# One queue for all transfers, the first four units' factors spread by TensorE, ScalarE's table loaded first

## The chip, the cores and the metric

The kernel runs on one core of a Trainium2 chip. The metric is the time of one execution on the device in microseconds; three runs of the kernel before are given, and one more execution was recorded by the hardware profiler. Engines are named as the profile names them: PE is TensorE (PEld its weight loads), DVE is VectorE, ACT is ScalarE, POOL is GpSimd, SP is SyncE. SPq and ACTq are the instruction queues of SP and ACT where they issue transfers.

## What is computed

A chunked linear-attention scan over 4 batches, 8 heads and 768 positions feeds two feed-forward layers with weights given in float64.

```python
# attention, per batch and head, chunk by chunk
log_a = np.log(np.clip(a, 1e-06, 1.0))
...
M = CB * L                      # L: products of the factors a between j and i, causal
y_intra = np.einsum('bhij,bhjd->bhid', M, xc)
y_inter = np.einsum('bhin,bhnd->bhid', Cc, state) * decay_to_i[:, :, :, None]
y[:, :, sl] = y_intra + y_inter
state = decay_full[:, :, None, None] * state + np.sum(Bx, axis=2)
...
# layer 1: rms norm, gate and value (256 -> 1536), silu(g) * val @ w_out (1536 -> 256)
silu = g * (1.0 / (1.0 + np.exp(-g)))
return (silu * val @ w_out).astype(np.float32)
...
# layer 2: 256 -> 2048 -> 256
g = s * (r * r) + b             # r = relu(x @ w_in)
return (g @ w_out).astype(np.float32)
```

## The kernel before

The attention works in 32 **units**. A unit is one chunk of 48 positions for two batches (two batches of one pair; unit number c is step c // 2 of pair c % 2), all heads, on 128 partitions. Each unit passes five steps: `scan` (DVE builds the decay products of the factors a into `a_sb`), `gram` (32 small PE matmuls from `raw_bc` into `y`, then DVE multiplies by the decays into `m`), `outs` (32 small PE matmuls of `m` with the inputs `xh`, then ACT copies to `yt`), `back` (PE transposes `yt`, ACT hands the state rows to the unit two later and squares, DVE and POOL make the norm factor `rs`, the scaled rows go to `xn`) and `turn` (PE transposes `xn`; the columns land in `xth`, and, from block 1 on, also in `xtl`). Four units make a block of 384 tokens, and there are eight blocks.

The weights arrive as float64 and are decoded on the chip: 12 tiles `w1[m]` of 768 KB (`load1`, `decode1`) and 16 tiles `w2[m]` of 512 KB (`decode2`). A decode is five DVE instructions and two ACT activations (the names `e`, `sg`, `raw`, then `w1f`). Buffers for raw `w1` tiles are three, so the load of tile m+3 waits for the decode of tile m.

Block 0 runs through layer 1 in plain float32 while the weights arrive (`hidden1_plain`): for tile i the first half of the block's columns (units 0 and 1) is taken as soon as the tile is decoded, and the second half (units 2 and 3) three tiles later. All later phases use three matmuls per product on a split into high and low parts.

What orders the work is a planner, the class `Plan`. Every instruction is recorded (`add`, with its dependences); `issue` then runs a list scheduler over all engines with prices from `price`, and writes the instructions out engine by engine in the order found. All computing instructions stand on one line, 306, in the profile; tiles tell them apart. Where the planner sees a hole on PE before the first layer-1 output it fills it with `idle` matmuls on a constant (line 302).

Transfers have two queues: SP's for most, and ACT's for the weight tiles and for the first `raw_bc` loads of units 0 and 1 (`load_bc`, `load1`, `decode2`). A transfer issued on ACT stands in ACT's own instruction order, so ACT does nothing else while one waits. The transfers of both queues share eight completion counters (DMAHW0 to DMAHW7 in the order rows below), taken in turn; a transfer waits on its counter until the earlier one on it has landed.

The factors reach a unit's partitions in three ways. Units 0 and 1 (`NCLIP = 2`) load raw factors broadcast over 64 partitions (`raw_a`, 128 KB each, two per unit) and clip them on DVE. At the same time all factors are loaded once into `a_cl`, clipped, and written to the scratch `a_scr` in HBM. Units 2 and 3 load theirs broadcast from `a_scr` (98 KB each, two per unit), later units in transfers for two steps at a time (196 KB).

Of the kernel before, what the change touches and what calls it, by code (L numbers as in the profile page):

```python
# [19 lines left out]
P = 128  # L20
# [3 lines left out]
NH = 8  # L24
# [4 lines left out]
NPAIR = 2  # L29
NUNIT = CPB * NPAIR  # L30
SLOTS = 2 * NPAIR
AW = CH + 1
# [6 lines left out]
DM = 256  # L39
NCLIP = 2  # L40
SIZE = {F32: 4, F32R: 4, I32: 4, U32: 4, BF16: 2, I16: 2, U16: 2, I64: 8}
# [11 lines left out]
class Plan:  # L53
# [18 lines left out]
    def __init__(self, nc):  # L72
        self.nc, self.ops, self.clock, self.pace = nc, [], 0.0, False
        self.seen, self.rings, self.masks, self.before = {}, {}, {}, {}
        self.closed, self.sent = set(), None
        for e in ("tensor", "vector", "scalar", "gpsimd", "sync"):
            setattr(self, e, Engine(self, e))

    def add(self, eng, fn, args, kw):
        op = dict(eng=eng, fn=fn, args=args, kw=kw, preds={}, paced=self.pace, i=len(self.ops))  # L80
        op["dur"] = self.price(eng, fn, args, kw)
        if fn == "dma_start":
            op["eng"] = "dma" if eng == "sync" else "words"
        reads = [a for k, a in kw.items() if k not in self.WRITES] + list(args)
        writes = [a for k, a in kw.items() if k in self.WRITES]
        if args and fn in self.FIRST_OUT:
            writes.append(reads.pop(len(kw) - len(writes)))
        for a in reads:
            self.touch(op, a, False)
        for a in writes:  # L90
            self.touch(op, a, True)
        if op["eng"] == "words":

            if self.sent is not None:
                op["preds"].setdefault(self.sent["i"], -self.DMA_LEAD - self.sent["dur"])
            self.sent = op
        op["clock"] = self.clock
        op["group"] = kw["out"].name if fn == "matmul" and not self.pace else None
        if self.pace:
            self.clock += op["dur"]  # L100
        self.ops.append(op)
# [45 lines left out]
    def need(self, op, o):  # L147
        if o is not op:
            lag = 0.0 if o["eng"] == op["eng"] == "tensor" else self.SEM_OF.get(o["eng"], self.SEM)
            op["preds"][o["i"]] = lag + (self.DMA_TAIL if o["eng"] in ("dma", "words") else 0.0)  # L150

# [35 lines left out]
    def queue_of(self, op):  # L187
        return "scalar" if op["eng"] == "words" else op["eng"]


    def forward(self, succs, late):
# [12 lines left out]
        def able(i):  # L204
            return max(ready[i], flights[-self.FLIGHTS]) if ops[i]["eng"] in ("dma", "words") else ready[i]

        for _ in ops:
# [6 lines left out]
            if pick is None:  # L214
                for n, i in enumerate(queue):
                    if able(i) > now + 1e-9:
                        continue
                    end = now + (self.DMA_ISSUE if ops[i]["eng"] == "words" else self.lasts(ops[i], now))
                    if e == "dma" or not any(
# [10 lines left out]
            start[pick] = now  # L230
            if op["eng"] in ("dma", "words"):
# [19 lines left out]
    def backward(self, succs, start, end):  # L251
# [8 lines left out]
        for _ in ops:  # L260
# [3 lines left out]
            free[e] = now + ops[i]["dur"]  # L264
            done = free[e] + (self.DMA_LEAD if e in ("dma", "words") else 0.0)
            late[i] = end - done
# [6 lines left out]

    def issue(self, idle):
        ops = self.ops
# [17 lines left out]
        _, start, stop = min(found, key=lambda f: f[0])  # L293

        ones = self.nc.const_aps.tensor(1.0, (P, P), BF16)
        until = min(start[op["i"]] for op in ops if getattr(op["kw"].get("out"), "name", None) == idle.name)
        busy = self.BEGIN
        for op in sorted(ops, key=lambda o: (start[o["i"]], o["i"])):
            i = op["i"]
            if op["eng"] == "tensor" and start[i] <= until:  # L300
# [3 lines left out]
                busy = stop[i]  # L304
            engine = getattr(self.nc, {"dma": "sync", "words": "scalar"}.get(op["eng"], op["eng"]))
            getattr(engine, op["fn"])(*op["args"], **op["kw"])  # L306
# [13 lines left out]
def scan_glu_relu2(ctx: ExitStack, tc: tile.TileContext, bc, xr, aa, cst, w1, w2, gn, sv, bv, out):  # L320
# [29 lines left out]
    mhalf, emin = fixed[:, 0:1], fixed[:, 1:2]  # L350
    a_cl = att1.tile([P, 4, R], F32, tag="yt", name="a_cl")
    a_scr = dram.tile([2 * NUNIT, NH * AW], F32, name="a_scr")
# [11 lines left out]
    def load_a(c):  # L364
        step, p = c // NPAIR, c % NPAIR
        t = a_t[c] = a_sb[:, c % SLOTS]
        for z in range(2):
            rows = slice(z * R, (z + 1) * R)
            if c < NCLIP:
                if z == 0:  # L370
                    raw = att2.tile([P, NH, R], F32, tag="m", name="raw_a")
                    nc.gpsimd.memset(t[:, :, 0:1], 0.0)
                nc.sync.dma_start(out=raw[rows].rearrange("p h r -> p (h r)"),
                                  in_=aa[chunk(c, z)].partition_broadcast(R))
            elif step == 1:
                nc.sync.dma_start(out=t[rows].rearrange("p h r -> p (h r)"),
                                  in_=a_scr[chunk(c, z)].partition_broadcast(R))
            elif step % 2 == 0:
                src = a_scr[chunk(c, z)]
                nc.sync.dma_start(  # L380
                    out=a_sb[rows, p::NPAIR].rearrange("p s h r -> p s (h r)"),
                    in_=bass.AP(src.tensor, src.offset, [[0, R], [NH * AW, 2], [1, NH * AW]]),
                )
        if c < NCLIP:
            clip_a(t[:, :, 1:AW], raw[:, :, 1:AW])
# [361 lines left out]

    o_t[0, 1] = new_o()
    tokens_to(1)
    for c in range(NPAIR):  # L750
        load_bc(c)
        load1(c)
    clip_a(a_cl[:, :, 1:AW], a_cl[:, :, 1:AW])
    nc.sync.dma_start(out=a_scr.rearrange("c (u h r) -> (c u) h r", u=2, h=4), in_=a_cl[:, :, 0:AW])
# [36 lines left out]
    with tc.manual_schedule():  # L791
        nc.issue(o_t[0, 1][0][:, :P])

# [70 lines left out]
```

## Time and profile before

| | us |
|---|---|
| three runs: lowest, median, highest | 682.12, 685.0, 685.35 |
| the profiled execution, its own time | 682.58 |
| its span, first to last instruction | 680.8 |
| PE busy | 657.7 (97%) |
| DVE busy | 390.6 (57%) |
| ACT busy | 351.8 (52%) |
| DMA moved | 36.14 MB, mean 53 GB/s |

The profiled execution's own time is 1.78 us above its span. Matmuls are pipelined and their ends are modelled, so "PE busy" says that PE had work, not that it worked at its peak. The `idle` matmuls count as busy.

### The profile page before, as it was taken

To read this page: it belongs to the slowest core of one execution; us is meant where nothing else is said; L and a number is where in the kernel's file an instruction comes from. 1 tells how busy PE (TensorE), PEld (TensorE's weight loads), DVE (VectorE), ACT (ScalarE), POOL (GpSimd) and SP (SyncE) were. 2 spreads that over 40 slices of the span, in tenths; PEclk is the share of its full clock that TensorE was granted. 3 is DMA by queue.
4 is the path that set the end of the run, shared out by engine and by line. 5 is a ranking of instruction groups with operands and counts; after the bars stand their busy time and mean duration, and the time that the engine had idled before them with its cause. 6 is when DMAs were issued, how large, how long until landed. Compare 5 with 4: busy or idle time off the path is not lost.

```text
span 680.8 us, 14058 instructions
## 1 busy us (share of the span) xinstructions
PE 657.7 (97%) x5569; PEld 630.8 (93%) x5569; DVE 390.6 (57%) x849; ACT 351.8 (52%) x790; POOL 34.7 (5%) x90
## 2 busy tenths in 40 slices
PE   4689999999999999999999999999999999999997
PEld 3579989899999989999999989999899999999997
DVE  2679999999944573345633465344733454334343
ACT  0778745876645553356533564345533554344553
POOL 3010010100000010000100010000100000000000
PEclk9999999999999999999999999999999999999999
DMA  6796792400001030001200031000400000000000
GB/s 143 206 206 231 230 264 106 97 6 0 7 1 25 7 92 24 0 7 29 73 22 1 7 95 26 1 7 7 92 24 1 6 2 25 1 1 1 4 21 25
DMA packets 26962, 36.14 MB, mean 53 GB/s; under 512 B 13840, under 2 KB 21008, under 8 KB 26896
## 3 DMA queue, kind: packets, MB, share of 16 engines
q1 hardware_dynamic: 22480, 16.89, 10.8%
q10 hardware_dynamic: 4416, 18.35, 8.6%
q8 instruction: 44, 0.72, 0.4%
q14 instruction: 22, 0.18, 0.1%
HBM read 31.98 MB, written 3.25 MB: 52 GB/s over the span
## 4 chain that ended last, share of the span: by engine, by line
PE 89%; DMA 6%; DVE 2%; ACT 1%; issue 1%; SPq 0%; ACTq 0%; POOL 0%; DVEq 0%; POOLq 0%
PE h L306 49%; PE o L306 34%; PE y L306 6%; DMA raw<-in_w 3%; DMA raw_a<-in_aa 1%; DMA a_sb<-a_scr 1%; DMA a_cl<-in_aa 1%; DVE a_sb L306 0%; SPq L306 0%; DVE m L306 0%; ACT L306 0%; ACT sg L306 0%; ACT s L306 0%; DVE e L306 0%; PE o L302 0%
## 5 line engine op out<-in xcount | busy, mean ns | idle before, releaser
L306 ACT ACTIVATE s<-h 128x384 f32<-128x384 f32 x212 | 104.4, 492 | 161.0 <-PE h L306 101.7
L306 PE MATMUL h<-x,w2hl 128*128 128x384 f32 x768 | 164.1, 341 | 0.0
L306 DVE TENSOR_TENSOR lo<-s,hi 128x384 fp32r<-128x384 f32 x212 | 118.0, 557 | 48.2 <-ACT hi L306 37.6
L306 PEld LDWEIGHTS h<-x,w2hl 128*128 128x128 f32 x768 | 135.9, 188 | 1.3
L306 PE MATMUL o<-hi,w2hl 128*128 128x384 f32 (+1 forms) x512 | 133.6, 342 | 0.0
L306 PE MATMUL h<-xtl,w1h 128*128 128x384 f32 x336 | 113.9, 340 | 0.9 <-DVE xtl L306 0.8
L306 PE MATMUL h<-xth,w1h 128*128 128x384 f32 x336 | 114.7, 341 | 0.0
L306 PE MATMUL h<-xth,w1l 128*128 128x384 f32 x336 | 113.7, 338 | 0.0
L306 DVE CAST hi<-s 128x384 fp32r<-128x384 f32 x128 | 45.8, 358 | 104.5 <-ACT s L306 91.5
L306 DVE TENSOR_TENSOR s<-h,s 128x384 f32<-128x384 f32 x84 | 46.7, 556 | 80.7 <-PE h L306 80.7
L306 PEld LDWEIGHTS o<-hi,w2hl 128*128 128x128 f32 x512 | 91.6, 188 | 1.2
L306 PE MATMUL o<-lo,w2hl 128*128 128x384 f32 (+1 forms) x256 | 87.8, 344 | 0.0
L306 ACT CAST hi<-s 128x384 fp32r<-128x384 f32 x84 | 43.1, 513 | 75.9 <-DVE s L306 75.7
L306 ACT ACTIVATE s<-s 128x384 f32<-128x384 f32 x128 | 67.2, 525 | 3.8
L306 PEld LDWEIGHTS h<-xtl,w1h 128*128 128x128 f32 x336 | 63.1, 188 | 1.8 <-DVE xtl L306 1.8
L306 PEld LDWEIGHTS h<-xth,w1h 128*128 128x128 f32 x336 | 63.1, 188 | 0.8 <-DVE h L306 0.2
L306 PEld LDWEIGHTS h<-xth,w1l 128*128 128x128 f32 x336 | 63.1, 188 | 0.2
L306 PE MATMUL o<-hi,w1h 128*128 128x384 f32 x168 | 57.1, 340 | 0.8 <-ACT hi L306 0.8
L306 PE MATMUL o<-hi,w1l 128*128 128x384 f32 x168 | 57.0, 339 | 0.0
L306 PE MATMUL o<-lo,w1h 128*128 128x384 f32 x168 | 56.9, 339 | 0.0
L306 POOL TENSOR_TENSOR rs<-ss,fixed 128x1 f32<-128x1 f32 x32 | 26.0, 811 | 461.2 <-DVE ss L306 461.2
L306 PEld LDWEIGHTS o<-lo,w2hl 128*128 128x128 f32 x256 | 48.1, 188 | 0.9
(65 smaller groups left out, 720.0 us busy)
## 6 DMA issues: line engine op xcount, KB each, us to landing
raw<-in_w ACTq DMA_DIRECT2D x12, 768.0 KB, 6.6
raw<-in_w ACTq DMA_DIRECT2D x16, 512.0 KB, 6.3
a_sb<-a_scr SPq DMA_DIRECT2D x28, 196.0 KB, 4.1
raw_bc<-in_bc SPq DMA_DIRECT2D x56, 64.0 KB, 3.8
xh<-in_xr SPq DMA_DIRECT2D x64, 48.0 KB, 3.0
out_t<-ob SPq DMA_DIRECT2D x14, 192.0 KB, 2.4
raw_a<-in_aa SPq DMA_DIRECT2D x4, 128.0 KB, 4.1
raw_bc<-in_bc ACTq DMA_DIRECT2D x8, 64.0 KB, 3.6
```

The costliest lines, as they stand in the source:

```text
L306: getattr(engine, op["fn"])(*op["args"], **op["kw"])
```

## The change

Four things are done.

1. Every transfer is issued by SP. `load_bc`, `load1` and `decode2` use `nc.sync`; the planner has one transfer queue "dma" in place of "dma" and "words". The weight tiles keep their order among themselves (`words` with the flag `turns`).
2. The first four units (`NCLIP = 2 * NPAIR`) take their factors from the one clipped tile `a_cl`: `spread_a` issues four PE matmuls per unit (out 64x196, the stationary operand a column of `ident` broadcast to 64 columns), which put the unit's factors on its partitions in a `ps_h` buffer of PSUM. The scan reads that buffer. The four `raw_a` loads, the four 98 KB `a_sb` loads, two clips on DVE and two memsets go away. `a_scr` is still written, for the later units.
3. `a_cl` is clipped before anything else, and gets a buffer of its own.
4. The first instruction on ACT is a Silu activation on one column of ones (`warm`).

```diff
-            op["eng"] = "dma" if eng == "sync" else "words"
+            op["eng"] = "dma"
...
-        if op["eng"] == "words":
+        if self.turns:
             if self.sent is not None:
                 op["preds"].setdefault(self.sent["i"], -self.DMA_LEAD - self.sent["dur"])
...
+        self.nc.scalar.activation(out=warm, in_=self.nc.const_aps.tensor(1.0, (P, 1), F32), func=AF.Silu)
...
-    a_cl = att1.tile([P, 4, R], F32, tag="yt", name="a_cl")
+    a_cl = const.tile([P, 4, R], F32, name="a_cl")
+    warm = const.tile([P, 1], F32, name="warm")
...
+    def spread_a(c):
+        ab = ps_h.tile([P, 512], F32, tag="h", name="ab")
+        v = ab[:, 0:NH * AW].rearrange("p (u h r) -> p u h r", u=2, h=4)
+        for u in range(2):
+            for z in range(2):
+                k = 2 * chunk(c, z) + u
+                nc.tensor.matmul(out=v[z * R:(z + 1) * R, u], lhsT=ident[:, k:k + 1].to_broadcast([P, R]),
+                                 rhs=a_cl[:, :, 0:AW], start=True, stop=True)
+        return ab[:, 0:NH * AW]
...
     def load_bc(c):
-        queue = nc.scalar if c < NPAIR else nc.sync
...
-                queue.dma_start(
+                nc.sync.dma_start(
...
         nc.vector.tensor_tensor_scan(
-            out=t, data0=t, data1=delta.rearrange("p h r -> p (h r)"),
+            out=t, data0=spread_a(c) if c < NCLIP else t, data1=delta.rearrange("p h r -> p (h r)"),
             initial=0.0, op0=ALU.mult, op1=ALU.add,
         )
...
+    def words(out, src):
+        nc.turns = True
+        nc.sync.dma_start(out=out, in_=src)
+        nc.turns = False
...
-        nc.scalar.dma_start(out=raw1[m], in_=w1[m])
+        words(raw1[m], w1[m])
...
-        nc.scalar.dma_start(out=raw, in_=w2[m])
+        words(raw, w2[m])
...
     o_t[0, 1] = new_o()
+    clip_a(a_cl[:, :, 1:AW], a_cl[:, :, 1:AW])
     tokens_to(1)
```

What the planner makes of it is seen in three places. The first is ACT's beginning, before: `raw_bc` are the first loads of units 0 and 1, `raw1` weight tiles, `yt` of unit 0 is the first computing step.

```order
L306 DMA raw_bc_103<-in_bc 16x2x512 x2
L306 DMA raw_bc_103<-in_bc 16x2x512 [waits DMAHW0_49]
L306 DMA raw_bc_103<-in_bc 16x2x512 [waits DMAHW4_49]
L306 DMA raw1_127<-in_w1 128x768 [waits DMAHW7_49]
L306 DMA raw_bc_103<-in_bc 16x2x512 [waits DMAHW4_49]
L306 DMA raw_bc_103<-in_bc 16x2x512 [waits DMAHW7_49]
L306 DMA raw_bc_103<-in_bc 16x2x512 [waits DMAHW0_49]
L306 DMA raw_bc_103<-in_bc 16x2x512 [waits DMAHW2_49]
L306 DMA raw1_128<-in_w1 128x768 [waits DMAHW5_49]
L306 ACT_TABLE_LOAD [waits DVE_49]
L306 COPY yt_134<-y_129 128x2x2x64 [waits PE_49]
L306 ACTIVATE sg_151<-raw1_127 128x768
```

And ACT's beginning in the changed kernel.

```order
L295 ACT_TABLE_LOAD
L295 ACTIVATE warm_111<-const-float32-1.0 128x1
L308 COPY yt_135<-y_130 128x2x2x64 [waits DVE_49,PE_49]
L308 ACTIVATE sg_153<-raw1_128 128x768 [waits DMAHW7_49]
L308 ACTIVATE xn_137,ss_138<-y_130 128x256 [waits PE_49]
```

Ten transfers that stood ahead of `yt` are gone from ACT, and the table load stands first; the program before has a second table load further down, the changed one has this one alone. Where they went is SP's beginning in the changed kernel (`xh_132` and `xh_133` are the inputs of units 0 and 1).

```order
L308 DMA a_cl_110<-in_aa 128x256
L308 DMA raw_bc_103<-in_bc 16x2x512 x4
L308 DMA xh_132<-in_xr 48x256 x2
L308 DMA raw1_128<-in_w1 128x768
L308 DMA raw_bc_103<-in_bc 16x2x512 [waits DMAHW0_49]
L308 DMA raw_bc_103<-in_bc 16x2x512 [waits DMAHW1_49]
L308 DMA raw_bc_103<-in_bc 16x2x512 [waits DMAHW2_49]
L308 DMA raw_bc_103<-in_bc 16x2x512 [waits DMAHW3_49]
L308 DMA xh_133<-in_xr 48x256 [waits DMAHW4_49]
L308 DMA xh_133<-in_xr 48x256 [waits DMAHW5_49]
L308 DMA raw1_129<-in_w1 128x768 [waits DMAHW6_49]
L308 DMA raw1_171<-in_w1 128x768 [waits DMAHW7_49]
```

SP began before with `raw_a`, then `a_cl`, `raw_a`; now `a_cl` is first, the first weight tile is the eighth transfer, and unit 1's `raw_bc` stand behind that tile in the same queue. The third place is PE from the end of its first `idle` matmuls (30 of them before, 24 now) to unit 0's first transposes, in the changed kernel. `ab_127`, `ab_136`, `ab_145` are the spreads of units 0, 1 and 2; `y_130` is unit 0, `y_140` unit 1.

```order
L308 MATMUL ab_127<-a_cl_110,ident_108 64x196 x3
L308 MATMUL y_130<-raw_bc_103 64x64 [waits DMAHW1_49,Pool_49]
L308 MATMUL y_130<-raw_bc_103 64x64 [waits DMAHW2_49]
L308 MATMUL y_130<-raw_bc_103 64x64 [waits DMAHW3_49]
L308 MATMUL ab_136<-a_cl_110,ident_108 64x196 x4
L308 MATMUL y_130<-raw_bc_103 64x64 [waits DMAHW4_49]
L308 MATMUL y_130<-raw_bc_103 64x64 x12
L308 MATMUL ab_145<-a_cl_110,ident_108 64x196 [waits DVE_49]
L308 MATMUL ab_145<-a_cl_110,ident_108 64x196 x3
L308 MATMUL y_130<-m_131,xh_132 32x64 [waits DMAHW5_49,DVE_49]
L308 MATMUL y_130<-m_131,xh_132 32x64 [waits DMAHW6_49,Pool_49]
L308 MATMUL y_130<-m_131,xh_132 32x64 x14
```

Three spreads now stand ahead of unit 0's `outs`. The fourth (`ab_158`) stands between unit 1's `gram` and its `outs`, and behind unit 1's first transposes there are 34 `idle` matmuls in a row, where before there were 5, the `gram` of unit 2 and 13.

## Rows read from the trace of the kernel before

**Rows 1.** The page's second part: PE's busy tenths in 40 equal slices of the span.

```profile
PE   4689999999999999999999999999999999999997
```

**Rows 2.** Busy time by stretch: length, PE, PEld, DVE, ACT, POOL, granted clock, DMA share, GB/s.

```profile
0.00:54.13 54.13, 36.73 (x473) 30.43 (x474) 31.55 (x60) 28.21 (x59) 9.46 (x30) 1.00 0.75 188
54.13:95.00 40.87, 40.87 (x422) 38.40 (x423) 40.06 (x86) 30.25 (x70) 3.71 (x4) 1.00 0.78 232
95.00:100.00 5.00, 4.17 (x47) 3.67 (x49) 4.11 (x8) 2.39 (x6) 0.00 (x0) 1.00 1.03 319
100.00:676.80 576.80, 575.89 (x4643) 558.29 (x4635) 314.86 (x698) 290.27 (x657) 21.52 (x56) 1.00 0.10 25
...
14.95:54.13 39.18, 29.57 (x374) 24.70 (x375) 28.97 (x55) 28.21 (x59) 3.91 (x4) 1.00 0.79 203
...
40.00:45.00 5.00, 4.55 (x26) 4.04 (x26) 4.43 (x8) 3.86 (x10) 1.19 (x1) 1.00 1.01 172
```

**Rows 3.** Timeline of ACT: start us, us, engine, operation, out<-in, count [idle before <-releaser].

```profile
0.74 4.62 ACTq L306 DMA_DIRECT2D raw_bc<-in_bc  x4
...
7.17 0.36 ACTq L306 DMA_DIRECT2D raw<-in_w  x1
...
7.57 10.11 ACTq L306 DMA_DIRECT2D raw_bc<-in_bc  x4
...
18.82 1.28 ACT L306 ACT_TABLE_LOAD   x1 [18.82 <-DMA a_sb<-a_scr]
20.11 0.37 ACT L306 COPY yt<-y 128x256 f32<-128x256 f32 x1
```

**Rows 4.** Timeline from the factors to unit 0's outputs, and the first layer-1 matmul.

```profile
1.41 0.57 SPq L306 DMA_DIRECT2D a_cl<-in_aa  x1
...
5.53 0.38 DVE L306 TENSOR_SCALAR a_cl<-a_cl 128x192 f32<-128x192 f32 x1 [5.53 <-DMA a_cl<-in_aa]
...
6.83 0.97 DVE L306 TENSOR_TENSOR_SCAN a_sb<-a_sb,delta 128x392 f32<-128x392 f32 x1
...
8.67 0.76 DVE L306 TENSOR_TENSOR m<-y,a_sb 128x384 f32<-128x384 f32 x2 [0.87 <-PE y L306]
...
9.48 0.78 PE L306 MATMUL y<-m,xh 64*32 64x64 f32 x32 [0.52 <-DVE m L306]
...
32.05 1.01 PE L306 MATMUL h<-xth,w1f 128*128 128x192 f32 x2
```

**Rows 5.** Timeline of PE: equal or like work at different places.

```profile
28.33 1.57 PE L302 MATMUL o<-const-bfloat16-1.0 128*128 128x128 bf16 x13
...
30.98 1.13 PE L306 MATMUL y<-raw_bc 16*64 16x64 f32 x32
...
33.27 2.77 PE L306 MATMUL h<-xth,w1f 128*128 128x192 f32 x8
...
59.51 1.46 PE L306 MATMUL h<-xth,w1f 128*128 128x192 f32 x8
```

**Rows 6.** The weights' feed: waits for a tile, landing times, PE's last wait for one.

```profile
14.95 0.56 DVE L306 TENSOR_SCALAR e<-raw 128x768 uint16<-128x768 uint16 x1 [5.52 <-DMA raw<-in_w]
...
39.61 0.36 DVE L306 TENSOR_TENSOR h<-h,h 128x192 f32<-128x192 f32 x1 [1.08 <-ACT h L306]
...
43.19 0.56 DVE L306 TENSOR_SCALAR e<-raw 128x768 uint16<-128x768 uint16 x1 [0.53 <-DMA raw<-in_w]
...
49.09 0.56 DVE L306 TENSOR_SCALAR e<-raw 128x768 uint16<-128x768 uint16 x1 [1.14 <-DMA raw<-in_w]
...
54.13 2.84 PE L306 MATMUL h<-xth,w1f 128*128 128x192 f32 x16 [0.16 <-DVE w1f L306]
...
DMA to landing us min/median/max: 3.9/6.4/9.7
```

**Rows 7.** Timeline where layer 1 changes to its second block.

```profile
98.66 0.50 ACT L306 CAST hi<-s 128x384 fp32r<-128x384 f32 x1
...
99.22 0.44 PE L306 MATMUL o<-hi,w1h 128*128 128x384 f32 x1 [0.82 <-ACT hi L306]
```

More of the change, by code (lines that the diff above doesn't have):

```diff
@@ L30 @@
 NUNIT = CPB * NPAIR
+NCLIP = 2 * NPAIR
 SLOTS = 2 * NPAIR
@@ L39 @@
 DM = 256
-NCLIP = 2
 SIZE = {F32: 4, F32R: 4, I32: 4, U32: 4, BF16: 2, I16: 2, U16: 2, I64: 8}
@@ L74, in __init__ @@
         self.seen, self.rings, self.masks, self.before = {}, {}, {}, {}
-        self.closed, self.sent = set(), None
+        self.closed, self.sent, self.turns = set(), None, False
         for e in ("tensor", "vector", "scalar", "gpsimd", "sync"):
@@ L149, in need @@
             lag = 0.0 if o["eng"] == op["eng"] == "tensor" else self.SEM_OF.get(o["eng"], self.SEM)
-            op["preds"][o["i"]] = lag + (self.DMA_TAIL if o["eng"] in ("dma", "words") else 0.0)
+            op["preds"][o["i"]] = lag + (self.DMA_TAIL if o["eng"] == "dma" else 0.0)
     def price(self, eng, fn, args, kw):
@@ L187, in queue_of @@
     def queue_of(self, op):
-        return "scalar" if op["eng"] == "words" else op["eng"]
+        return "gpsimd" if op["eng"] == "sync" else op["eng"]
     def forward(self, succs, late):
@@ L204, in able @@
         def able(i):
-            return max(ready[i], flights[-self.FLIGHTS]) if ops[i]["eng"] in ("dma", "words") else ready[i]
+            return max(ready[i], flights[-self.FLIGHTS]) if ops[i]["eng"] == "dma" else ready[i]
         for _ in ops:
@@ L217, in forward @@
                         continue
-                    end = now + (self.DMA_ISSUE if ops[i]["eng"] == "words" else self.lasts(ops[i], now))
+                    end = now + self.lasts(ops[i], now)
                     if e == "dma" or not any(
@@ L230, in forward @@
             start[pick] = now
-            if op["eng"] in ("dma", "words"):
+            if e == "dma":
                 done = carried = max(now + self.DMA_LEAD, carried) + op["dur"]
@@ L264, in backward @@
             free[e] = now + ops[i]["dur"]
-            done = free[e] + (self.DMA_LEAD if e in ("dma", "words") else 0.0)
+            done = free[e] + (self.DMA_LEAD if e == "dma" else 0.0)
             late[i] = end - done
@@ L272, in backward, with issue @@
         return late
-    def issue(self, idle):
+    def issue(self, idle, warm):
         ops = self.ops
@@ L304, in issue @@
                 busy = stop[i]
-            engine = getattr(self.nc, {"dma": "sync", "words": "scalar"}.get(op["eng"], op["eng"]))
+            engine = getattr(self.nc, op["eng"] if op["eng"] != "dma" else "sync")
             getattr(engine, op["fn"])(*op["args"], **op["kw"])
@@ L365, in load_a @@
         step, p = c // NPAIR, c % NPAIR
[L366 to L378, printed above, removed]
+        a_t[c] = a_sb[:, c % SLOTS]
+        if c >= NCLIP and step % 2 == 0:
+            for z in range(2):
                 src = a_scr[chunk(c, z)]
                 nc.sync.dma_start(
-                    out=a_sb[rows, p::NPAIR].rearrange("p s h r -> p s (h r)"),
+                    out=a_sb[z * R:(z + 1) * R, p::NPAIR].rearrange("p s h r -> p s (h r)"),
                     in_=bass.AP(src.tensor, src.offset, [[0, R], [NH * AW, 2], [1, NH * AW]]),
                 )
-        if c < NCLIP:
-            clip_a(t[:, :, 1:AW], raw[:, :, 1:AW])
+    def spread_a(c):
+        ab = ps_h.tile([P, 512], F32, tag="h", name="ab")
+        v = ab[:, 0:NH * AW].rearrange("p (u h r) -> p u h r", u=2, h=4)
+        for u in range(2):
+            for z in range(2):
+                k = 2 * chunk(c, z) + u
+                nc.tensor.matmul(out=v[z * R:(z + 1) * R, u], lhsT=ident[:, k:k + 1].to_broadcast([P, R]),
+                                 rhs=a_cl[:, :, 0:AW], start=True, stop=True)
+        return ab[:, 0:NH * AW]
     def load_bc(c):
-        queue = nc.scalar if c < NPAIR else nc.sync
         for z in range(2):
@@ L752, in scan_glu_relu2 @@
         load1(c)
-    clip_a(a_cl[:, :, 1:AW], a_cl[:, :, 1:AW])
     nc.sync.dma_start(out=a_scr.rearrange("c (u h r) -> (c u) h r", u=2, h=4), in_=a_cl[:, :, 0:AW])
@@ L791, in scan_glu_relu2 @@
     with tc.manual_schedule():
-        nc.issue(o_t[0, 1][0][:, :P])
+        nc.issue(o_t[0, 1][0][:, :P], warm)
 def kernel(**inputs):
```

## The prediction

> **What bounds the kernel now.** I read the page's slices first: PE is busy in nine tenths or more of every slice from the fourth on [rows 1]. The table by stretch then says where the holes are [rows 2]: up to 54.13 us PE has work for 36.73 us; from 54.13 to 95 it never stops, between 95 and 100 it loses 0.83 us, and from 100 to 676.8 it loses 0.9 us in 577. So the end of the program follows PE, and whatever brings PE to the state that it has at 54.13 us earlier brings the end forward by as much, as long as nothing new stalls it later. The change acts on those first 54 us and on the stall at 98 us.
>
> Within them the timeline of ACT shows the first cause [rows 3]: ACT issues four `raw_bc` loads from 0.74, a weight tile at 7.17, and four more loads that take from 7.57 to 17.7, because each waits for one of the eight counters. Behind them stands the table load at 18.82, and only then, at 20.11, the copy `yt`. Its input, the last `outs` matmul of unit 0, was there at 9.48 + 0.78 = 10.26 [rows 4]. ACT thus held unit 0 for 9.85 us, and unit 1's `gram` was stuck behind unit 0's transposes on PE. The first layer-1 matmul runs at 32.05 [rows 4]. From there PE waits for decoded tiles, the last time at 54.13 [rows 6].
>
> PE also runs slowly here. The granted clock column reads 1.00 in every stretch [rows 2], but eight rows of `h` take 2.77 us at 33.27 and 1.46 us at 59.51 [rows 5]: by its durations PE was at the lower of its two levels (1.2 GHz) at 33 us and at the upper one (2.4 GHz) later.
>
> **The change part by part.** I sum against the profiled execution: 680.8 us of span, 682.58 of its own time. That is 2.4 us under the median of the three runs (685.0), which lie in a pair and a single one; I apply the gain to both and take the middle, 683.8, as the start.
>
> *Unit 0 up to `yt`.* `a_cl` was issued at 1.41 and its clip began at 5.53, 4.12 later [rows 4]. It now goes first, at 0.74, where the queues start [rows 3]: clip at 4.86, done 0.38 later at 5.24, PE starts near 5.4. POOL's set-up of `ident` and `delta` runs beside that. A spread is four float32 matmuls of 196 columns on 64 output rows, which this trace doesn't have. The nearest row is four float32 matmuls (eight rows) of 192 columns on 128 output rows, 2.77 us at the lower level [rows 5]; one after another the spread is 2.77 x 196/192 = 2.8 us. The other end is half, 1.4 us, if the two 64-row halves run side by side. I take 1.4, since the small matmuls do that: 32 `outs` rows of 64 columns take 0.78 us [rows 4], 24 ns each. With 1.4: spread 0 to 6.8, spread 1 to 8.2, the `gram` (1.13 for 32 rows at the lower level [rows 5]) to 9.3; the scan of unit 1, 0.97, now stands on DVE ahead of `m` and runs to 9.4; `m` 0.76 to 10.2; spread 2 meanwhile to 10.7; `outs` 0.78 to 11.5 [rows 4]. `yt` starts near 11.6 instead of 20.11. With 2.8 the same chain gives 8.2, 11.0, 12.1, `m` done at 12.9, spread 2 to 14.9, `outs` to 15.7, `yt` at 15.8. A scan that reads PSUM is not in the trace either; for 0.97 us I allow 0.1 either way, within the rounding.
>
> *From `yt` to the first layer-1 matmul*: 32.05 - 20.11 = 11.94 us before. New in it is spread 3 between unit 1's `gram` and `outs`, 1.4 to 2.8 us, of which the 0.76 of `m` hides as much: +0.7 (0 to +2.0). The run of 34 `idle` matmuls stands where 18 stood; at 1.57/13 = 0.12 us each [rows 5] the 16 more are 1.9 us, beside unit 1's norm chain: +1.0 (0 to +1.9). The order puts the first layer-1 matmul straight behind unit 1's transposes, ahead of unit 3's `gram`, 1.13: -1.1. Net +0.6 (-1.1 to +2.8). First layer-1 matmul: 11.6 + 11.94 + 0.6 = 24.1, **7.9 us earlier**; the ends are 22.4 (9.6 earlier) and 30.5 (1.5 earlier).
>
> *Is the first tile there by then?* Seven transfers go ahead of it on SP; at 0.57 us an issue, the longest shown [rows 4], it is issued at 4.7 and lands 3.9 to 9.7 later, 6.4 by the median [rows 6]: 11.1, where its decode began at 14.95 before [rows 6]. The decode is beside the unit chain, so this costs nothing up to 24.1. Unit 1's `raw_bc` now follow that tile in one queue and are wanted by PE near 12: 0 if the tile lands by the median, up to +1.5 if it lands at 13. I take +0.7.
>
> The Trainium skill (DMA: Bandwidth & Descriptors, Queues, rings and completion order) speaks against this part: each DMA engine takes turns between the queues that have work, a packet at a time, so that a small load on a second queue slips in between the packets of a tile, while on one queue it stands behind all of it. By that rule the `raw_bc` cost would be the upper end, +1.5, and the sum 0.8 us smaller. No row here separates the two, since unit 1's loads waited for counters.
>
> *The tiles after that.* DVE waited 0.53 and 1.14 us for tiles 4 and 5, and 1.08 us for an activation behind the second table load [rows 6]. ACT no longer issues, and the table is loaded while `a_cl` is under way, so 1.08 goes; the four `raw_a` and four 98 KB loads (0.9 MB) are off the DMA engines. All three waits gone is -2.75; nothing gained is 0, since every load now stands in one in-order queue. I take **-1.5**. The clips that go (two on DVE) and the POOL memsets lie beside waits: nothing.
>
> The Trainium skill (ScalarE: Activation LUTs, What ACT_TABLE_LOAD costs) prices a table load with its drain at 2.66 us. The trace differs: the load takes 1.28 and the copy starts 0.01 later [rows 3], so the measured value holds. By the page's price this term would be 1.4 us larger.
>
> *The stall at 98 us.* PE waited 0.82 us for the cast `hi`, which ran late on ACT at 98.66 [rows 7], in a stretch where ACT issued weight tiles. These go to SP: **-0.8** (0 to -0.83).
>
> *Everything later* keeps its work. PE's order has the same matmuls, and the waits left are small [rows 2].
>
> Sum: -7.9 + 0.7 - 1.5 - 0.8 = **-9.5 us**: 671.3 of span, 673.1 beside the profiled execution, 675.5 beside the median, 674.3 from the middle. The good ends (-9.6, 0, -2.75, -0.83) give -13.2; the bad ends (-1.5, +1.5, 0, 0) give 0.
>
> **The rivals.**
>
> *Tiles one at a time.* On SP the fourth tile waits for the third one's landing, and small loads and the later tiles queue behind that wait. If each tile from the third on is issued only when the one before it has landed, then with the third issued at 11.1, when the first lands, the sixth lands four landings later: at the median of 6.4 us at 36.7, in time; at 9.7 us [rows 6] at 49.9, where it was at 49.09 before. Then only the 0.8 is left: 683.0, no change. For it speaks that the DMA engines were full (share 1.01) at 172 GB/s from 40 to 45 us [rows 2]; against it, that these 5 us also carried broadcast loads for later units, part of which now go earlier.
>
> *Serial spreads.* PE takes 2.8 us per spread and stays at the lower level: first layer-1 matmul at 30.5. 1.5 + 1.5 + 0.8 = 3.8 us gained: 680.0. Against it: side-by-side rows in `outs`, and a busier PE, which tended to the upper level after 33 us.
>
> *Decoding is the bound.* DVE decodes without a pause from 54 to 95 (40.06 of 40.87 us [rows 2]). If DVE's 10.2 idle us between 14.95 and 54.13 [rows 2] stay, all moves only with the first tile, 14.95 - 11.1 = 3.85, plus 0.8: 4.7 gained, 679.1. Against it: most of that idling lies in the wait for ACT, which goes.
>
> *Slower: second-layer tiles ahead of a unit's loads.* SP's order now has ten `w2` tiles of 512 KB ahead of unit 8's `raw_bc` and `a_sb`, some 5.7 MB. At the 232 GB/s of 54 to 95 us [rows 2] that is 25 us, which I take as the time that PE has until unit 8's `gram`. At 167 GB/s it is 34 us, and the 9.5 us are gone: from there the kernel is slower. At 140 GB/s it is 41 us, 16 late, 6.5 slower: 690. For it: the 172 GB/s row. Against: that row has small broadcasts; 95 to 100 us, with tiles mostly, shows 319 [rows 2].
>
> That the change doesn't do what it says is excluded for the issuing: the order shows ACT with no transfer and one table load.
>
> **How the numbers follow.** Forecast, 674.3: 0.68. Tiles one at a time, 683: 0.10. Serial spreads, 680: 0.10. Decoding the bound, 679.1: 0.07. Slower, 690: 0.05. The range reaches from the good ends beside the profiled execution, 669.5, to just past the serial spreads, 680.3; 0.15 of the rivals' chance lies above, and a little of the forecast outside. A measurement of this kernel can tell about 0.5%, 3.4 us. Faster by more: the forecast, decoding, and most of the serial spreads (3.8 gained), 0.83. Within it: 0.12. Slower: 0.05.
>
> **What would show it.** In the profile after: `yt` of unit 0 starting between 11 and 13 us; spreads of about 1.4 us; a first layer-1 matmul near 24; PE's last wait for a decoded tile near 44 instead of 54; no hole at 98 shifted by 9.5; 0.8 to 1 us of PE idle after that. A `yt` at 16 or spreads near 2.8 us mean serial spreads. DVE waits for tiles of several us between 25 and 45 mean tiles one at a time. A PE wait for `raw_bc` or a scan's `a_sb` near 80 to 100 us means the second-layer tiles. I am wrong at the root if `yt` comes early and the first layer-1 matmul doesn't.

## The result, and the profile after

The kernel after takes 674.78 us (median of 4 runs, 674.42 to 677.3), the kernel before on the same chip 685.17 (4 runs, 682.12 to 685.35): a ratio of 0.9867, with an interval of 0.983 to 0.9903. It is faster by 10.4 us between the medians. The profiled execution is the longest of its four, 677.3 us with a span of 675.4; the spans of the other three are 672.5 to 673.2. That of before was short for its kernel. Between the two traces lie therefore only 5.4 us (680.8 and 675.4 of span), and what follows accounts for these; the rest of the 10.4 lies between executions that no trace shows.

The page's second part, PE's busy tenths and granted clock in 40 slices of the span, to be held against [rows 1]: the first three slices read 0.8, 0.7 and 0.9 instead of 0.4, 0.6 and 0.8, and the clock row has a 0.8, a 0.9 and a 0.6 there.

```profile
PE   8799999999999999999999999999999999999997
...
PEclk8969999999999999999999999999999999999999
```

The timelines of ACT, DVE and PE at the start (start, us, operation; in brackets the idle time before it and its releaser) answer to [rows 3] and [rows 4].

```profile
0.73 1.28 ACT L295 ACT_TABLE_LOAD   x1 [0.73 <-PEq L860]
...
8.94 0.37 ACT L308 COPY yt<-y 128x256 f32<-128x256 f32 x1 [6.71 <-PE y L308]
```

```profile
2.98 0.50 DVE L308 TENSOR_SCALAR a_cl<-a_cl 128x192 f32<-128x192 f32 x1 [2.98 <-DMA a_cl<-in_aa]
4.97 0.97 DVE L308 TENSOR_TENSOR_SCAN a_sb<-ab,delta 128x392 f32<-128x392 f32 x1 [1.49 <-POOL delta L308]
...
9.57 0.56 DVE L308 TENSOR_SCALAR e<-raw 128x768 uint16<-128x768 uint16 x1 [0.47 <-DMA raw<-in_w]
...
32.76 0.56 DVE L308 TENSOR_SCALAR e<-raw 128x768 uint16<-128x768 uint16 x1 [4.17 <-DMA raw<-in_w]
...
38.43 0.56 DVE L308 TENSOR_SCALAR e<-raw 128x768 uint16<-128x768 uint16 x1 [1.72 <-DMA raw<-in_w]
```

```profile
3.58 0.88 PE L308 MATMUL ab<-a_cl,ident 128*64 128x196 f32 x8
...
5.67 0.88 PE L308 MATMUL ab<-a_cl,ident 128*64 128x196 f32 x8
...
10.03 0.85 PE L308 MATMUL y<-raw_bc 16*64 16x64 f32 x4 [1.20 <-DMA raw_bc<-in_bc]
...
12.48 1.57 PE L308 MATMUL ab<-a_cl,ident 128*64 128x196 f32 x8
...
20.18 0.59 PE L308 MATMUL h<-xth,w1f 128*128 128x192 f32 x2 [0.43 <-ACT xth L308]
...
34.83 0.69 PE L308 MATMUL y<-ident,xn 128*128 128x128 f32 x2 [4.24 <-ACT xn L308]
...
41.99 2.74 PE L308 MATMUL h<-xth,w1f 128*128 128x192 f32 x8
...
45.22 1.46 PE L308 MATMUL h<-xth,w1f 128*128 128x192 f32 x8
...
47.17 1.46 PE L308 MATMUL h<-xth,w1f 128*128 128x192 f32 x8
```

ACT now waits for PE before `yt` and not for its own transfers: `yt` starts at 8.94 instead of 20.11, and the first layer-1 matmul stands at 20.18 instead of 32.05, 11.87 us earlier. Not all of this lead stays. At 34.83 PE has been idle for 4.24 us, waiting for `xn` from ACT, and the eight rows of `h` at 41.99 take 2.74 us, the same rows at 45.22 take 1.46. Of the 192 rows of `h` of block 0 (a float32 matmul stands as two), the 57th started at 54.13 before [rows 6] and is now the first of the group at 47.17: 7 us of the 11.87 are left. The table by stretch (length, PE, PEld, DVE, ACT, POOL, granted clock, DMA share, GB/s) shows the same.

```profile
30.00:35.00 5.00, 0.76 (x5) 0.46 (x4) 1.90 (x3) 2.21 (x6) 0.00 (x0) 0.92 1.05 225
35.00:45.00 10.00, 10.00 (x89) 8.57 (x90) 6.32 (x11) 6.51 (x14) 0.00 (x0) 0.53 0.79 216
```

After idling, PE runs at a granted clock of 0.53, the lower level (1.2 GHz), for some ten microseconds. Why it idled stands in ACT's timeline and in the chain of waits: the fifth weight tile was issued at 23.09 and landed 9.65 us later, DVE and `sg` on ACT wait for it, and `xn`, which needs nothing from the tile, stands behind `sg` on ACT.

```profile
27.95 0.22 ACT L308 ACTIVATION_READ_ACCUMULATOR xn<-y 128x1 f32 x1
32.76 0.92 ACT L308 ACTIVATE sg<-raw 128x768 bf16<-128x768 int16 x1 [4.59 <-DMA raw<-in_w]
33.56 0.72 ACT L308 COPY xh<-y 16x256 f32<-16x256 f32 x2
34.30 0.47 ACT L308 ACTIVATE xn<-y,rs 128x256 f32<-128x256 f32 x1
```

```profile
23.09 9.65 DMA raw<-in_w
```

After that PE never stops up to 100 us; the hole of [rows 7] is gone. With it the lead is 7.73 us at a cast of the second phase, 137.52 against 145.25 before. At the last output activation but one, 638.77 against 644.64, it is 5.87. The later phases have lost 1.86 us up to there.

```profile
137.52 0.48 ACT L308 CAST x<-o 128x384 fp32r<-128x384 f32 x1 [0.53 <-PE o L308]
...
638.77 1.24 ACT L308 ACTIVATE ob<-o,sb 128x384 f32<-128x384 f32 x2
```

### The profile page after: what moved, and what is told of

Read it like the earlier page. It is cut to its first block, busy times and chain, and to the rows that moved or that the text cites. A ratio compares the mean times of both kernels' runs of the same rounds, so it can differ in the third digit from the quotient of the medians.

```text
span 675.4 us, 14121 instructions
## 1 busy us (share of the span) xinstructions
PE 659.8 (98%) x5602; PEld 632.0 (94%) x5602; DVE 388.2 (57%) x847; ACT 349.0 (52%) x790; POOL 32.9 (5%) x88
## 3 DMA queue, kind: packets, MB, share of 16 engines
HBM read 31.05 MB, written 3.25 MB: 51 GB/s over the span
## 4 chain that ended last, share of the span: by engine, by line
PE 90%; DMA 5%; ACT 1%; issue 1%; SPq 1%; DVE 1%; ACTq 0%; DVEq 0%
PE h L308 50%; PE o L308 34%; PE y L308 6%; DMA a_sb<-a_scr 3%; DMA raw<-in_w 1%; SPq L308 1%; DMA raw_bc<-in_bc 1%; DVE xn L308 0%; ACT sg L308 0%; ACT w1h L308 0%; DVE m L308 0%; ACT xn L308 0%; ACT xh L308 0%; DVE hi L308 0%; ACT xth L308 0%
## 5 line engine op out<-in xcount | busy, mean ns | idle before, releaser
L308 POOL TENSOR_TENSOR rs<-ss,fixed 128x1 f32<-128x1 f32 x32 | 24.2, 755 | 457.8 <-DVE ss L308 457.8
```

## The experiments

Three theories stood at the start: that one queue for all transfers carries the gain (A), that the spreads carry it, or that the early table load does. Later ones ask what made the new hole and what the later phases lost. Each job ran the kernel before on its own chip; ratios are against that. They are the ratios on record and not quotients of the medians printed here: for the queue alone, below, the medians give 0.9913 and the record 0.9884. The first job's kernel before had a median of 683.69 (19 runs), the second's 686.0 (7), the third's 683.44 (17).

**The table load alone, in the kernel before.**

```diff
+        self.nc.scalar.activation(out=warm, in_=self.nc.const_aps.tensor(1.0, (P, 1), F32), func=AF.Silu)
```

> Part 4 alone: the kernel before with ScalarE's table loaded first. Transfers stay on both queues, factors as before. Theory A (the gain comes from freeing ScalarE of transfers; the table is a small extra): yt of unit 0 still starts behind ACT's transfers, at about 19 us instead of 20.11, since only the 1.28 us load goes from in front of it; the 1.08 us wait behind the second load goes too. 1 to 2.5 us faster than before. Rival B (the table loads stood on the path with their drain, so they carry much of the gain): 4 to 6 us faster. Rival C (the load now delays the first transfers on ACT by 1.3 us): no change.

Measured: 684.46 us, ratio 1.0005 (0.9971 to 1.004). No change; the 1 to 2.5 us that theory A expected did not come. The timeline of ACT shows why: the table is loaded at 0.73, and `yt` still starts at 20.42, behind four `raw_bc` issues that took 6.24 us.

```profile
13.34 6.24 ACTq L308 DMA_DIRECT2D raw_bc<-in_bc  x4
19.96 0.35 ACTq L308 DMA_DIRECT2D raw<-in_w  x1
20.42 0.37 ACT L308 COPY yt<-y 128x256 f32<-128x256 f32 x1 [18.19 <-DMA raw_bc<-in_bc]
```

**The queue alone.** The factors reach units 0 to 3 as before, and no table is loaded ahead.

```diff
-            engine = getattr(self.nc, {"dma": "sync", "words": "scalar"}.get(op["eng"], op["eng"]))
+            engine = getattr(self.nc, op["eng"] if op["eng"] != "dma" else "sync")
```

> Part 1 alone: every transfer issued by SP, the factors still loaded broadcast (raw_a for two units, 98 KB from scratch for two), table loads where they fall. Theory A (freeing ScalarE is the main part): yt of unit 0 near 11 to 13 us, first layer-1 matmul near 24 to 26 us, 6 to 9 us faster than before. Rival D (one queue only pays once the broadcast loads are gone, since they then stand in front of the weight tiles): yt early, but the decode of tiles and units 1 to 3 late, 0 to 4 us faster.

Measured: 677.72 us, ratio 0.9884 (0.9841 to 0.9927). Between the medians it is 5.97 us faster than the kernel before, just short of theory A's 6 to 9, where the kernel after is 10.39 and, in a later job, 8.16 us faster; the intervals of the ratios overlap. `yt` starts at 12.05, the first layer-1 matmul at 27.01. This kernel too has a hole at the weight tiles, PE 6.97 of 10 us from 30 to 40.

```profile
12.05 0.37 ACT L307 COPY yt<-y 128x256 f32<-128x256 f32 x1 [0.84 <-DMA a_scr<-a_cl]
```

```profile
30.00:40.00 10.00, 6.97 (x71) 5.78 (x69) 6.35 (x13) 7.15 (x19) 1.34 (x2) 0.98 0.77 232
```

**The spreads alone, transfers from both queues.**

```diff
-NCLIP = 2
+NCLIP = 2 * NPAIR
...
-            out=t, data0=t, data1=delta.rearrange("p h r -> p (h r)"),
+            out=t, data0=spread_a(c) if c < NCLIP else t, data1=delta.rearrange("p h r -> p (h r)"),
```

> Part 2 and 3 alone: the first four units' factors spread by TensorE from the one clipped tile, transfers still on both queues, table loads where they fall. Theory A: ACT is still held by its own transfers, yt near 15 to 18 us (fewer transfers share the eight counters), 1 to 4 us faster than before. Rival D (the spread is what pays): 6 us or more faster. Rival E (the spread's matmuls cost PE time and nothing else changes): no change to 2 us slower.

**The spreads and the early table load, transfers from both queues.**

```diff
+        self.nc.scalar.activation(out=warm, in_=self.nc.const_aps.tensor(1.0, (P, 1), F32), func=AF.Silu)
...
+NCLIP = 2 * NPAIR
```

> The kernel before with the spreads and the early table load, its transfers still issued from both queues. Theory A (without the move to one queue nothing is gained): yt well before 16.73 us, since the table is loaded, but the lead is lost again at 80 to 120 us to the second stall, and the time is that of before within 0.5%: 682 to 687, ratio 0.997 to 1.003. Rival F (the two edits need each other, and the queue is worth what they leave): 678 or less, ratio below 0.992.

Measured: 686.02 us, ratio 1.0025 (0.9997 to 1.0053), and 685.22, ratio 1.0022 (0.9994 to 1.0049). Neither gains. `yt` starts at 16.73 and 17.17, still behind ACT's own issues, and layer 1 begins some 5 us earlier than before; most of the lead is given back between 80 and 120 us, the rest after it. The 1 to 4 us that theory A expected of the spreads alone did not come, and the early table load did not bring `yt` forward. With spreads alone PE works 16.36 of 20 us there, where the kernel before has 19.18 and the kernel after 20.00, and ACT's timeline shows it held twice for the issue of a tile, 2.24 and 3.14 us, until another load had landed.

```profile
80.00:100.00 20.00, 16.36 (x171) 14.42 (x170) 12.59 (x26) 6.18 (x19) 0.55 (x1) 0.91 1.01 249
100.00:120.00 20.00, 19.27 (x102) 19.21 (x103) 19.33 (x39) 11.52 (x22) 0.00 (x0) 0.91 0.32 107
```

```profile
85.59 0.33 ACTq L306 DMA_DIRECT2D raw<-in_w  x1
85.97 0.33 ACT L306 ACTIVATE h<-h 128x192 f32<-128x192 f32 x1 [2.24 <-DMA a_sb<-a_scr]
...
99.18 0.34 ACTq L306 DMA_DIRECT2D raw<-in_w  x1
99.56 0.49 ACT L306 ACTIVATE s<-h 128x384 f32<-128x384 f32 x1 [3.14 <-DMA a_sb<-a_scr]
```

So nothing is gained without the queue, and the queue alone gains. The table load was a victim of the transfers that stood ahead of it. What the spreads bring beside the queue is not settled: no run on one chip compares the two. The queue alone has a median of 677.72; with the spreads added, and still no early table load, the next experiment has 672.58 and 672.62, on chips where the kernel before had 686.0 and 683.44 against 683.69 here. A gain of some 5 us by the spreads beside the queue, 0.7%, fits these runs. On the chip of the queue alone the nearest is the kernel with eight spread units and the early load, further down, with 675.06.

**The kernel after without the early table load.** It was run twice, the second time beside the kernel after itself.

```diff
-        self.nc.scalar.activation(out=warm, in_=self.nc.const_aps.tensor(1.0, (P, 1), F32), func=AF.Silu)
```

> The kernel after without the early table load; everything else is as in the kernel after. Theory A (the gain is ACT's freedom from transfers, the table load was only a victim of them): ACT loads the table when its first function comes up, right before yt of unit 0, so yt starts 1.28 us later, near 10.2 instead of 8.94, the first layer-1 matmul near 21.5 instead of 20.18, and since PE then waits for the fifth tile until 32.76 anyway, the time stays within 1 us of the kernel after: 674 to 677, ratio 0.985 to 0.990. Rival C (the early table is worth its own microseconds): yt more than 3 us later and 678 or more.

> The kernel after without the early table load, once more, beside the kernel after on the same chip. Theory A: within 0.5% of it (3.4 us) either way. Rival C2 (the table load at 9.3 us, when yt's input is not yet there, is cheaper than the one at 0.73, as 672.58 against 674.78 in different chip jobs would say): 2 us or more under the kernel after.

> The kernel after, unchanged, beside the next three on one chip. Theory A (the queue gives the gain, the early table load nothing): 672 to 676, the same as the kernel without the early table load within 0.5%. Theory H (PE's stall at 31 to 35 us is what the loads of units 4 to 7 cost in every execution): a DVE wait of 2 us or more for the fifth tile near 30 us, and PE below 9 of 10 us between 30 and 40. Rival I (that stall was bad luck of the one execution profiled): no such wait.

Measured: 672.58 us (ratio 0.9819, 0.9773 to 0.9865) the first time, less than either theory had it, with `yt` at 10.67 and the first layer-1 matmul at 20.5. Then, on one chip, 672.62 without the early load (0.984, 0.9801 to 0.988) and 675.28 with it (0.9885, 0.9845 to 0.9924). The early load brings nothing; without it the median was lower by 2.66 us, 0.4%, which is under what the measurement can tell and fits theory A and rival C2 alike, though both jobs point the same way. The hole is no accident of one execution: it is there again in the second trace of the kernel after, where the fifth tile took 9.20 us. Both traces are of long executions (677.3, the longest of four, and 677.1, the second longest of six); whether the others have it, no trace shows. The second trace and one without the early load, in this order, show what differs.

```profile
30.00:35.00 5.00, 1.29 (x7) 0.66 (x6) 2.50 (x5) 2.84 (x6) 0.00 (x0) 0.94 1.05 248
35.00:40.00 5.00, 5.00 (x44) 4.33 (x44) 2.99 (x6) 3.23 (x9) 0.00 (x0) 0.50 0.90 210
```

```profile
30.00:35.00 5.00, 4.42 (x53) 3.36 (x51) 3.48 (x6) 3.90 (x11) 1.76 (x1) 1.00 1.06 268
35.00:40.00 5.00, 4.57 (x57) 3.85 (x50) 3.55 (x7) 3.55 (x6) 0.00 (x0) 1.00 0.87 235
```

ACT's timeline in the latter:

```profile
8.30 1.28 ACT L307 ACT_TABLE_LOAD   x1 [8.30 <-DVE m L307]
```

```profile
23.19 1.28 ACT L307 ACT_TABLE_LOAD   x1
...
29.70 0.93 ACT L307 ACTIVATE sg<-raw 128x768 bf16<-128x768 int16 x1
```

ACT loads a table twice, at 8.30 while `yt`'s input isn't there yet, and at 23.19. It comes to the fifth tile at 29.70 and finds it landed; with the early load it was done at 28.14 and waited 3.98 us, until 32.12. PE then waits little at a time, and its granted clock stays at 1.00 from 30 to 40 us. Why that tile landed earlier (the DMA engines moved 268 GB/s at a share of 1.06 there, against 248 at 1.05) is not settled. A late tile alone doesn't make the hole, though. In the other trace without the early load (of the run with 672.58) the fifth tile took nearly as long as in the kernel after and held `sg` until 31.53, and still PE waited only 0.17 us before the same transposes, at 33.63.

```profile
22.61 8.90 DMA raw<-in_w
```

```profile
25.82 0.46 PE L307 MATMUL y<-m,xh 64*32 64x64 f32 x32 [2.00 <-DVE m L307]
26.21 3.25 PE L307 MATMUL h<-xth,w1f 128*128 128x192 f32 x10
```

The second table load, here at 23.32, had held ACT and with it PE: ten rows of `h` that started at 24.68 in the kernel after and took 1.94 us start at 26.21 and take 3.25. PE still had work when the tile landed. In these traces the hole takes both, a late tile and a PE that is early.

**Eight spread units instead of four.** Units 4 to 7 no longer load `a_sb` from the scratch while the weight tiles arrive.

```diff
-NCLIP = 2 * NPAIR
+NCLIP = 4 * NPAIR
```

> The changed kernel with eight units spread instead of four (NCLIP = 4 * NPAIR): the four 196 KB broadcast loads of units 4 to 7 go, 16 more spread matmuls come. In the changed kernel PE stands idle from 30.6 to 34.8 us and slows to its lower level after it, because weight tile 4 takes from 23.1 to 32.7 us to land. Theory S1 (the DMA engines are full with the units' broadcast loads then): tile 4 lands 3 to 5 us earlier, the hole is gone or under 1.5 us, 2 to 6 us faster than the changed kernel, 12 to 16 us faster than before. Rival S2 (the three raw buffers and the waits in one queue make the tiles late): tile 4 takes as long, the hole stays, and the kernel is 0 to 2 us slower than the changed one for 2.8 us more matmuls.

Measured: 675.06 us (673.23 to 678.45), ratio 0.9852 (0.9807 to 0.9896). The hole is gone, DVE and ACT wait for no tile there, and the cast that stood at 137.52 stands at 132.33, although PE has four more spreads to do.

```profile
30.00:35.00 5.00, 5.00 (x88) 4.35 (x87) 5.00 (x9) 5.00 (x11) 0.00 (x0) 1.00 0.66 213
35.00:45.00 10.00, 10.00 (x65) 9.44 (x65) 10.00 (x20) 8.01 (x14) 0.00 (x0) 1.00 0.67 225
```

The four 196 KB broadcasts thus made the tiles late: without them the fifth tile, issued at 22.09, is there when ACT comes to it at 27.82, and the DMA share from 30 to 35 us falls from 1.05 to 0.66. But the median is not lower than that of the kernel after; the 2 to 6 us expected did not come. The two traces don't show why. Of the 5.2 us won at the cast they keep 4.2 at the last output activation but one (634.57 against 638.77), but one is of the shortest of its four executions and the other of the longest. What they show is a smaller loss in the later phases: from the cast to that activation it is 502.24 us, against 501.25 in the kernel after and 499.39 in the kernel before. PE's waits in the stretch from 130 to 660 us (total, times, longest) name the place.

```profile
PE h L308 <- DVE xtl L308: 3.0, 4, 1.1
```

**Later scans in the plan.** The scans on DVE wait for an `a_sb` 2.4 us between 130 and 660 us in the kernel before, 6.3 in the kernel after and 5.2 with eight spread units. Broadcast loads of `a_sb` had medians to landing of 4.7 us (60 to 100 us, the kernel after) to 9.0 us (the same stretch, spreads alone); behind 100 us it was 3.8 in the kernel before, 4.3 in the kernel after and 4.4 with eight units. The planner counts on 3.8 us: by its constants 1.7 of lead, 0.6 for 196 KB, 1.3 of tail and 0.2 for the semaphore. The kernels with eight and with four spread units were built with 3 us more between the two, and the first of them also without the early table load.

```diff
             op["preds"][o["i"]] = lag + (self.DMA_TAIL if o["eng"] == "dma" else 0.0)
+            if o["fn"] == "dma_start" and o["kw"]["out"].name.startswith("a_sb"):
+                op["preds"][o["i"]] += 3.0
```

> The kernel with eight spread units and, in the planner, 3 us more between the landing of a broadcast load of a_sb and the scan that reads it, so that the plan counts on the 6 us that such loads took. Theory D (the 2.8 us that phases after 200 us lose there are PE waits for xtl, behind scans whose a_sb landed late): PE's waits for xtl fall from 3.0 us to under 1 us, the markers' lead of 12.9 us at 132 us holds to the end, and the time is 1.5 to 3 us under that of the kernel with eight spread units: 672 to 673.5, ratio 0.980 to 0.983. Rival E (PE's waits there have another cause, or the later place of the scan makes PE wait instead): 675 or more, ratio above 0.985.

> The kernel after with the same 3 us in the planner for the a_sb loads. Theory D: the first 60 us keep their hole at 31 to 35 us or have a smaller one, since the scans of units 4 to 7 stand later too; the 2 us that the later phases lost go, and the time is 672.5 to 674. Rival E: no change against the kernel after, 674 to 676, or more where the scans of units 4 to 7 come too late for their gram: up to 678.

> Eight spread units and 3 us more in the planner for a_sb loads, without the early table load. Theory A and D: 670 to 672, ratio 0.977 to 0.983, as with the early table load (670.84). Rival C2: 669 or less.

Measured: 670.84 us (670.58 to 671.83), ratio 0.9793 (0.9755 to 0.983), with eight spread units. With four, 672.45 (0.9816, 0.9777 to 0.9854). With eight and no early table load, 671.38 (0.9819, 0.9786 to 0.9853). The theory on the late loads holds in the traces: with eight and with four alike neither PE nor a scan has a wait left between 130 and 660 us. What this alone is worth in time is not settled, since these kernels and those with the old plan ran on different chips, and the new plan changes the start too: with four units the first layer-1 matmul is at 18.90 instead of 20.18 and PE's wait for `xn` is 2.43 us instead of 4.24. The table by stretch for the later phases, first of the kernel after, then with eight spread units and later scans:

```profile
200.00:400.00 200.00, 198.82 (x1791) 189.94 (x1790) 96.56 (x224) 95.80 (x230) 8.11 (x13) 1.00 0.14 32
400.00:665.00 265.00, 264.12 (x1963) 257.89 (x1963) 119.70 (x267) 121.14 (x274) 6.44 (x9) 1.00 0.07 15
```

```profile
200.00:400.00 200.00, 200.00 (x1831) 191.72 (x1830) 99.23 (x231) 98.43 (x240) 7.74 (x12) 1.00 0.14 33
400.00:665.00 265.00, 264.42 (x1940) 258.89 (x1938) 119.76 (x263) 121.23 (x268) 5.12 (x8) 1.00 0.06 14
```

The last output activation but one of this kernel stands 497.62 us behind its second-phase cast (134.81 to 632.43), 4.6 us less than with eight units and the old plan, and its runs lie within 1.25 us instead of 5.2. The start is slower here than with the old plan (134.81 against 132.33), so the lead isn't the 12.9 us that theory D wanted held, but grows from 10.4 to 12.2 us. The two kernels with eight units and later scans have the lowest medians of all; on one chip 671.38 stands against 675.28 of the kernel after, 0.6% less. They can't be told apart from one another.

**The layer-2 tiles back on ACT, in the kernel after.**

```diff
+            if op["eng"] == "dma" and op["kw"]["out"].name.startswith("raw2"):
+                engine = self.nc.scalar
```

> The kernel after with only the w2 tiles issued by ACT again, each at its planned place. The w1 tiles and all small loads stay on SP. Theory A2 (PE's stall at 98 us of the kernel before comes from ACT being held by the tiles that it issues): the casts of the first result, back to back at 91.54 in the kernel after, come apart again, PE is below 19 of 20 us between 80 and 100 us, and the time is 1 to 5 us longer than the kernel after: 676 to 680. Rival B2 (the stall came from what the DMA engines carry there, whatever queue the tiles are in): no new stall, 674 to 676. Rival B3 (tiles in a second queue leave unit 8's loads the first one, which helps): up to 2 us shorter, 672.5 to 674.

Measured: 675.62 us, ratio 0.9854 (0.9813 to 0.9894). No stall: PE works 20.00 of 20 us from 80 to 100. ACT is held once, 1.79 us before a cast, and PE doesn't notice.

```profile
89.50 0.34 ACTq L310 DMA_DIRECT2D raw<-in_w  x1
89.88 0.86 ACT L310 CAST x<-o 128x384 fp32r<-128x384 f32 x2 [1.79 <-DMA raw<-in_w]
```

So issuing these tiles on ACT isn't enough for the stall of [rows 7]. In this kernel ten of them go out between 54 and 70 us, in the kernel after between 54 and 72, and the DMA share from 80 to 100 is 0.63; where the stall was there it was 1.02 (before) and 1.01 (spreads alone). That the stall needs both, ACT as the issuer and full DMA engines, fits these four traces; it was not tried by itself. A fourth buffer for raw `w1` tiles, which would let the fifth tile be issued earlier, wasn't tried.

## Why the prediction was right, and where not

The forecast of 674.3 and the measured 674.78 agree, and the first cause is the one named: ACT held unit 0 for its own transfers, and taking these away brings PE forward. The terms agree less well than the sum, and the sum was made for the two traces, where it failed: 9.5 us forecast, 5.4 measured.

- *Unit 0 up to `yt`*, forecast 8.5 us earlier, measured 11.17. Two sizes were off. `a_cl` was in 2.2 us after its issue (0.74 to 2.98) and not 4.12. It landed the later the more went beside it: 2.7 us behind one `raw_a` in one queue (the queue alone), 3.0 first on SP with `raw_bc` loads on ACT (spreads and early table load), 4.1 before, with both. A spread took 0.88 us and not 1.4: the granted clock was 1.00 there, the upper level, where the nearest row, eight rows on 128 output rows, takes 1.46 [rows 5], so one after another it would have been 1.49. The one spread at the lower level, at 12.48 (granted clock 0.50), took 1.57, near the 1.4 that had been taken and far from 2.8. Serial spreads are refuted. POOL's set-up did not run wholly beside this, as the sum had it: the first scan waited 1.49 us for `delta`, until 4.97.
- *From `yt` to the first layer-1 matmul*, forecast 12.5, measured 11.24. The first layer-1 matmul came 11.9 us earlier, beyond the good end of 9.6.
- *Unit 1's `raw_bc` behind the first tile*, forecast +0.7. PE waited 1.20 us for it, until 10.03, while the tile was being decoded from 9.57 on. The Trainium skill's rule on queues (DMA: Bandwidth & Descriptors, Queues, rings and completion order) would have the small load stand behind the whole tile in one queue; the two landings, half a microsecond apart, agree with that, and no run here has the same pair on two queues. The wait costs at most its 1.20 us and lies inside the 11.24.
- *The tiles after that*, forecast -1.5, the ends 0 and -2.75: here the prediction failed. From the first layer-1 row to the 57th the lead shrank from 11.87 to 6.96 us, so this term was **+4.9**. (Four rows of `o` that stood ahead of the 57th before stand behind it now, which would make it some 0.7 more.) The step took PE's waits for tiles to vanish or stay and didn't see that an earlier start brings layer 1 into the time when the broadcasts of units 4 to 7 fill the DMA engines. The tile took 9.65 us to land, as long as the 9.7 that the rival "tiles one at a time" was priced with, and the wait reached PE by a way not considered: `xn` behind `sg` on ACT, and then ten microseconds at the lower level. Eight spread units show that without the broadcasts the tile is in time; the kernel without the early table load shows that with them a PE that comes a little later has no hole. The tiles did not go one at a time: the sixth was issued at 27.07, before the fifth landed, and the rival's 683 did not come.
- *The rival "decoding is the bound"*, 679.1, is nearer to the traces than the forecast. Its condition, that DVE's idle time stays, came true: 10.4 of the 37.6 us between the first decode, at 9.57, and the 57th row, where it was 10.2 of 39.18. Most of its waits for ACT went, the longest 4.56 us, and waits for tiles came, 4.17 and 1.72 us. The first decode moved by 5.38 us (14.95 to 9.57). Its 4.7 us stand beside the 5.4 between the traces; only the medians, 10.4 apart, speak for the forecast.
- *The stall at 98 us*, forecast -0.8: gone. The cause given, ACT issuing weight tiles, is not shown: with the layer-2 tiles back on ACT the stall stayed away.
- *Everything later*, forecast unchanged: it lost 1.86 us in the profiled execution. PE waits 2.1 us between 130 and 660 us, 1.2 more than before, behind scans whose `a_sb` landed late; the remaining 0.6 or so is no wait of PE and stays open. Whether the late loads also spread the runs is not shown.
- *Slower through layer-2 tiles ahead of unit 8's loads*: no. PE waits for nothing from 80 to 100 us.

Two errors of 4.7 and 6.4 us (a start that came sooner than the sum had it, the `raw_bc` term included, and tiles that came later) thus cancelled for the most part, and the later loss is another 1.9. Of the signs named, only the missing hole at 98 us came as said: `yt` and the first layer-1 matmul came earlier than said, the spreads were shorter, and PE's last wait behind a tile ended at 34.83 and not near 44, and was 4.24 us long. That the median still fell where the sum put it is luck in good part: it owes this to the cancelling and to the spread of the runs, since the traced execution of before was short for its kernel and that of after long. The queue was right as the part without which nothing is gained: alone it has a ratio of 0.9884.

## What to carry to other kernels

A transfer issued by a computing engine puts its wait for a completion counter into that engine's order; moved to an engine that computes nothing it gave 1.2% here by the ratio (0.9% by the medians), while edits that only shortened what stood behind it gave nothing without the move. When a start moves forward by 12 us, look up which transfers then meet the same stretch, and which unrelated instructions stand behind the waits that grow. A load planned just in time should be planned with the landing time that the trace shows: 3 us more slack in the plan for one kind of load took away the last waits of PE.

## What was not expected of the hardware

- Four float32 matmuls of 196 columns onto 64 output rows, in two halves, took 0.88 us at the upper level and 1.57 at the lower, where one after another they would be 1.49 and 2.8 by the rows of like matmuls on 128 output rows.
- The 1.28 us table load at 23.19, in the middle of the work, did no harm: the kernel with two loads had a median 2.66 us below the one with a single early load, within what the measurement can tell.
- The granted clock column shows the lower level after the 4.24 us hole (0.50 from 35 to 44 us), while in the kernel before it read 1.00 where eight rows of `h` took 2.77 us [rows 5]: the durations have to be read beside it.
